# Early attention in buffers that weights take over one by one, a softmax in three instructions, and a scheduler that knows of DVE and GpSimd waiting for each other

## The chip, the cores and the metric

The kernel runs on one core of a Trainium2 chip. The metric is the device time of one execution in microseconds (us). PE is TensorE, DVE is VectorE, ACT is ScalarE, POOL is GpSimd, and SP is the engine from whose queue the kernel issues all its DMAs.

## The reference

Attention of 4 batches, 8 heads, 576 positions and 64 channels feeds two feed-forward layers on 2304 tokens.

```python
# attention: coarse part on means over 4 positions, plus a band of 7 neighbours
out_d = sm_attn(q_d, k_d, v_d)                   # 144 x 144 softmax per head
mask = np.abs(pos[:, None] - pos[None, :]) < 4
attn = softmax(np.where(mask, scale * q @ k.T, -1e9))
x = np.repeat(out_d, 4, axis=2) + attn @ v
# layer 1: RMS norm, gate, value, output (512 -> 1536 -> 512)
xn = x / rms * rms_g
x = (silu(xn @ w_gate) * (xn @ w_val)) @ w_out
# layer 2 (512 -> 2048 -> 512)
x = np.maximum(x @ w_in, 0) ** 2 @ w2_out
```

## The kernel before

No instruction is issued where the code stands. Each call of an engine is recorded as an `Op`; at the end `Plan.trace` puts all records in an order and emits them, which is why every row of the profile has the one line of the emitting call. The order comes from a list scheduler, `Plan.order`: it has a cost in us for each operation (`cost`), a delay between two engines (`lag`), and it alternates between forward and backward passes (`ROUNDS` of them, with a random share of `JIT` in the priorities, drawn from `SEED`), and keeps the order with the earliest end. Some records may run on one of several engines: `VP` on DVE or POOL, `AV` on ACT or DVE; the scheduler chooses. Nothing of this is a time on the chip. Each engine then takes its instructions strictly in the emitted order, and so does the DMA queue of SP.

The string `PLAN` sets in which sequence the parts are recorded:

- `d0` to `d15` (`down`): coarse attention of one batch and two heads. Loads q, k, v; sums over 4 positions on DVE; scores, softmax and output through PE, ACT and DVE. For batches 1 to 3 the result goes to DRAM (`od_d`).
- `a0` to `a5` (`wide`) and `b0` to `b5` (`wide_post`): the band for batch 0, 96 tokens at a time, on PE, with a softmax over 8 heads x 104 keys (tiles `wp`, `wnm`, `wsm`), then the norm into `xh`/`xl`, the input of layer 1.
- `u0` to `u13` and `p2` to `p8`: the band for batches 1 to 3, token rows on partitions: a product of k and q and one of v and the weights per row (tile `pr`, `VP`), summed on DVE; then the norm of a block of 256 tokens.
- `w00` to `w52`: loading and decoding a weight of layer 1. Weights arrive as 64-bit numbers in a staging tile `st` of 512 x 2 words and become two tiles, `hi` and `lo`, so that a product takes three matmuls. One half of a weight is one `decode`: ACT, DVE (two inputs), ACT or DVE, DVE, DVE, POOL or DVE (add), ACT or DVE (`hi`), POOL or DVE (`lo`, a subtraction).
- `x`: one step of layer 1 for a block of 256 tokens and 256 hidden units: 24 matmuls into bank `g`, 24 into `v`, 24 of the step before into `a` or `b`. ACT (`th`, `hh`) and DVE (`th`, `v`, `hl`) stand between them. These matmuls of split numbers are called block matmuls below.

After the last `x` come the weights of layer 2 (32 halves `w2i`, `w2o`) and its steps with 512 tokens.

On-chip memory: a pool `early` holds what the early attention needs (q, k, 7 tiles `wp`, and so on). The pools `late` (6 weights of layer 1 and the staging ring `s`) and `dn` take the same space after the mark `E` in `PLAN`; every first user of a `late` tile waits for every user of `early`. PSUM has 8 banks: tags `a` and `b` with two buffers, `g`, `v`, `t`, `d` with one.

Of the kernel before, what the change touches and what calls it, by code (L numbers as in the profile page):

```python
# [15 lines left out]
I32 = mybir.dt.int32  # L16
# [29 lines left out]
XAB = 2  # L46
DT = 'dbg'
DT1 = ['abt', 'dtd', 'add']
WS = 'aaabbb'
WPT = 'vvvddd'  # L50
WX = 'dtgggb'
WTP = 'ttattt'
VB = 3
PB = 7
NB = 1
DL = 1
EST = 2
SEQ = '011100001101'
PLAN = 'd3 d0 d1 d2 w00 a0 a1 b0 a2 b1 a4 b2 a3 w01 w12 b4 w10 w02 b3 a5 w11 w21 w30 w20 b5 d7 d5 d4 d6 u0 w22 E w31 u1 w32 w41 w40 w42 x x w51 w50 x x x x x x w52 x x x p2 x u2 d8 u3 p3 u4 x d10 x d11 u5 d9 x x x x p4 u6 x x d14 d13 x x d12 x u7 x p5 u8 x d15 x u9 x x x x p6 x x x u10 x u11 x x x p7 x u13 u12 x x x x p8 x x x x x x x x x x x x'
SLOT = [7, 6, 9, 8, 3, 4, 2, 0, 1, 5]  # L60
ROUNDS = 10
LOCK = False
W2ST = 6
# [3 lines left out]
SLACK = 0.02  # L67
JIT = 0.1
SEED = 68976

# [10 lines left out]
def cost(e, method, args, kw, out, ins):  # L81
# [10 lines left out]
    if e in "DQ":  # L92
        return max(0.45, 1.42e-3 * n)
    if e == "A":
# [147 lines left out]
class Op:  # L242


    def __init__(self, n):
        self.n, self.calls, self.cost, self.uses, self.held = n, {}, {}, {}, {}
        self.before, self.after = set(), []

# [11 lines left out]
class Plan:  # L260
# [64 lines left out]
    def record(self, names, method, args, kw):  # L325
# [10 lines left out]
        for e in names:  # L336
            op.calls.setdefault(e, []).append((method, args, kw))
            op.cost[e] = op.cost.get(e, 0.0) + cost(e, method, args, kw, out, ins)
            op.held[e] = e + "S" if LOCK and shared(e, method, kw, out, ins) else op.held.get(e, e)
        for views, writes in ((ins, False), (out, True)):  # L340
# [23 lines left out]
    def order(self, first, forth):  # L364
# [4 lines left out]
        free = defaultdict(lambda: BEGIN if forth else 0.0)  # L369
        done, starts, where, gate = {}, {}, {}, Gate()  # L370

# [18 lines left out]
        while len(done) < len(self.ops):  # L390
# [67 lines left out]
def attn_moe_kernel(ctx: ExitStack, tc, qs, kw, vw, qt, kt, vt, v4, wg, wv, wo, w2i, w2o, gw, gb,  # L458
# [95 lines left out]
    wq, wk, wod = [None] * 4, [None] * 4, [None] * 4  # L554
    qbds = [tile("early", f"qbd{i}", [128, 3, 2, 48]) for i in range(2)]

    def down(b, pr, tags):

        nq, nk = S + SD, S + 8 + SD
        if not late:  # L560
            pool, n = "early", NB
            if b == 0:
                q, k, v4s = (tile("w", f"w{n}", [128, 1024]) for n in (2 * pr, 2 * pr + 1, 8 + pr))
                q, k = q[:, 0:nq], k[:, 0:nk]
                v4s = v4s[0:72].rearrange("p (g d f) -> p g d f", g=4, f=4)
                wq[pr], wk[pr] = q, k
            else:
                q = tile("early", "q", [128, nq], F32, DL)
                k = tile("early", "k", [128, nk], F32, DL)
                v4s = tile("early", "v4s", [72, 4, 64, 4], F32, DL)  # L570
            qbd = qbds[pr % 2]
        else:
            pool, n = "dn", 1
# [3 lines left out]
            qbd = qbds[2]  # L577
# [21 lines left out]
        nm = tile(pool, "nm", [96, 3], F32, 2)  # L599
        V.tensor_reduce(out=nm, in_=sps, axis=AX.X, op=ALU.max, negate=True)  # L600
# [10 lines left out]
        with plan.joint():  # L611
            for h in range(2):
                for qc in range(2):
                    for kc in range(2):
# [29 lines left out]
    def wide(t):  # L644

        v = tile("early", "wv", [WK, DM], F32, VB)
        DQ.dma_start(out=v, in_=vt[WT * t:WT * t + WK])
        p = tile("early", "wp", [WT, 2, 4, WK], F32, PB)
        pt = tile("early", "wpt", [WK, 2, 4, WT], F32, VB)
        bd = band_sb[:, 0 if t == 0 else 2 if t == S // WT - 1 else 1].unsqueeze(1).to_broadcast([WT, 4, WK])  # L650
        sp = [bank(WS[t])[0:WT, 0:4 * WK].rearrange("p (r k) -> p r k", r=4) for h in range(2)]
        with plan.joint():
# [5 lines left out]
        for h in range(2):  # L658
            V.scalar_tensor_tensor(out=p[:, h], in0=sp[h], scalar=SCALE, in1=bd, op0=ALU.mult, op1=ALU.add)
        nm = tile("early", "wnm", [WT, 8], F32, 2)  # L660
        sm_ = tile("early", "wsm", [WT, 8], F32, 2)
        pf = p.rearrange("p h r k -> p (h r) k")
        V.tensor_reduce(out=nm, in_=pf, axis=AX.X, op=ALU.max, negate=True)
        for i in range(8):
            A.activation(pf[:, i], pf[:, i], AF.Exp, bias=nm[:, i:i + 1], accum_out=sm_[:, i:i + 1])
        V.tensor_scalar(out=sm_, in0=sm_, scalar1=1e-9, scalar2=None, op0=ALU.add)
        V.reciprocal(out=sm_, in_=sm_)
        VP.tensor_tensor(out=pf, in0=pf, in1=sm_.unsqueeze(2).to_broadcast([WT, 8, WK]), op=ALU.mult)
        for h in range(2):
            tp = bank(WPT[t])[0:WK, 0:4 * WT].rearrange("p (r k) -> p r k", r=4)  # L670
            with plan.joint():
# [5 lines left out]
    def wide_post(t):  # L677

        pt, v = wx.pop(t)
        x = bank(WX[t])[0:WT]  # L680
        with plan.joint():
# [9 lines left out]
        xa = tile("early", "wxa", [WT, DM], F32, 2)  # L691
        ss = tile("early", "wss", [WT, 1], F32, 2)
# [4 lines left out]
        tp = bank(WTP[t])[:, 0:4 * WT].rearrange("p (k n) -> p k n", k=4)  # L697
        with plan.joint():
# [417 lines left out]
```

## Time and profile before

| | before |
|---|---|
| time, median of 3 runs | 1038.81 us (1036.69 to 1041.39) |
| profiled execution: time | 1037.73 us |
| profiled execution: span from first to last instruction | 1036.0 us |
| mean granted clock of TensorE | 0.958 |
| PE / weight loads of PE | 975.4 us (94%) / 898.2 us (87%) |
| DVE / ACT / POOL | 614.4 (59%) / 414.6 (40%) / 443.8 us (43%) |

The span is 1.7 us shorter than the time of the same execution; the rest lies outside the first and last instruction. The engines' shares are means over stages that have little in common: attention and decoding at first, then matmuls almost alone, with a second stretch of decoding at about 560 to 700 us.

### The profile page before, as it was taken

How to read it: one execution, taken by the hardware profiler on the slowest of the kernel's cores; microseconds unless marked ns; L12 is line 12 of the kernel's file. 1: busy time of each engine (PE TensorE's matmuls, PEld its weight loads, DVE VectorE, ACT ScalarE, POOL GpSimd, SP SyncE). 2: the span in 40 equal slices, each digit the busy share in tenths (PEclk: the TensorE clock that was granted, in tenths of full speed). 3: DMA queues.
4: the chain of work that ended last, by engine and by line, in shares of the span. 5: the costliest groups of instructions: out<-in, count | busy, mean ns of one | idle time of the engine just before them, and what ended most of it. 6: DMA issues, size and time to landing. Idle time of an engine off the chain costs nothing.

```text
span 1036.0 us, 16567 instructions
## 1 busy us (share of the span) xinstructions
PE 975.4 (94%) x6540; PEld 898.2 (87%) x6540; DVE 614.4 (59%) x978; ACT 414.6 (40%) x984; POOL 443.8 (43%) x300
## 2 busy tenths in 40 slices
PE   4688988799999999999999899999999999999998
PEld 4588988799999999999999898777888888888897
DVE  6879999898766767666734578863322322222232
ACT  4678645544334242423223556663222322222222
POOL 0668688995644756568611456861000100000000
PEclk9656999899999999999999999999999999999999
DMA  9735473345343332412010346331100100100010
GB/s 248 200 109 164 134 241 103 100 137 175 102 130 111 93 120 73 127 62 92 27 32 11 133 140 207 99 125 61 72 1 1 52 1 0 41 1 1 1 41 21
DMA packets 38463, 92.89 MB, mean 90 GB/s; under 512 B 4218, under 2 KB 14498, under 8 KB 38386
## 3 DMA queue, kind: packets, MB, share of 16 engines
q1 hardware_dynamic: 38386, 91.84, 28.0%
q8 instruction: 51, 0.84, 0.3%
q14 instruction: 26, 0.21, 0.1%
HBM read 80.62 MB, written 11.21 MB: 89 GB/s over the span
## 4 chain that ended last, share of the span: by engine, by line
PE 61%; DVE 13%; POOL 9%; DMA 7%; issue 4%; ACT 4%; SPq 0%; DVEq 0%; POOLq 0%; ACTq 0%
PE v L454 17%; PE g L454 17%; PE a L454 14%; PE b L454 11%; DVE st L454 6%; POOL st L454 2%; POOL pr L454 2%; POOL w L454 2%; DMA st<-in_w2o 2%; ACT st L454 1%; DVE s L454 1%; DMA k<-in_kw 1%; PE d L454 1%; DMA w<-in_v 1%; DMA st<-in_w2i 1%
## 5 line engine op out<-in xcount | busy, mean ns | idle before, releaser
L454 PE MATMUL g<-xh,w 128*128 128x256 f32 (+1 forms) x1184 | 271.8, 309 | 4.1 <-DVE th L454 4.1
L454 PE MATMUL v<-xh,w 128*128 128x256 f32 (+1 forms) x1040 | 248.2, 316 | 15.6 <-DVE hl L454 14.9
L454 PEld LDWEIGHTS g<-xh,w 128*128 128x128 f32 x1184 | 200.7, 191 | 15.3 <-DVE th L454 5.0
L454 PEld LDWEIGHTS v<-xh,w 128*128 128x128 f32 x1040 | 181.4, 195 | 27.3 <-issue 14.9
L454 PE MATMUL g<-xl,w 128*128 128x256 f32 (+1 forms) x592 | 181.2, 306 | 0.0
L454 PE MATMUL v<-xl,w 128*128 128x256 f32 (+1 forms) x520 | 163.2, 314 | 0.0
L454 DVE SCALAR_TENSOR_TENSOR v<-v,th 128x512 f32<-128x512 f32 (+1 forms) x94 | 63.2, 673 | 134.9 <-ACT th L454 91.6
L454 POOL TENSOR_TENSOR pr<-v,es 128x896 f32<-128x896 f32 x54 | 100.4, 1942 | 68.8 <-DVE es L454 42.3
L454 ACT ACTIVATE th<-g 128x512 f32<-128x512 f32 (+1 forms) x94 | 54.3, 577 | 167.2 <-PE g L454 166.9
L454 PEld LDWEIGHTS g<-xl,w 128*128 128x128 f32 x592 | 113.2, 191 | 5.2
L454 POOL TENSOR_TENSOR pr<-k,q 128x896 f32<-128x896 f32 x49 | 106.5, 2192 | 21.6 <-DVE sc L454 12.9
L454 PEld LDWEIGHTS v<-xl,w 128*128 128x128 f32 x520 | 101.8, 196 | 5.3
L454 POOL TENSOR_TENSOR xl<-st,xh 128x1024 fp32r<-128x1024 f32 (+1 forms) x8 | 16.9, 2125 | 204.3 <-ACT xh L454 204.2
L454 ACT ACTIVATE st<-st 128x512 int32<-128x512 uint32 (+1 forms) x118 | 78.9, 682 | 58.6 <-DVE st L454 31.7
L454 ACT CAST hh<-v 128x512 fp32r<-128x512 f32 (+1 forms) x94 | 53.4, 568 | 109.6 <-DVE v L454 98.6
L454 DVE TENSOR_SCALAR st<-st 128x512 f32<-128x512 f32 (+1 forms) x118 | 87.2, 748 | 8.6 <-ACT st L454 6.7
L454 POOL TENSOR_TENSOR w<-st,w 128x512 fp32r<-128x512 f32 x55 | 78.1, 1427 | 28.7 <-ACT w L454 28.5
L454 PE MATMUL a<-w,hh 128*128 128x512 f32 x320 | 86.7, 392 | 2.4 <-ACT hh L454 2.4
L454 POOL TENSOR_TENSOR st<-st 128x512 int32<-128x512 int32 x59 | 71.1, 1208 | 38.8 <-DVE st L454 36.1
L454 DVE SCALAR_TENSOR_TENSOR g<-g,th 128x512 f32<-128x512 f32 (+1 forms) x40 | 25.8, 644 | 99.6 <-ACT th L454 99.6
L454 DVE TENSOR_TENSOR hl<-v,hh 128x512 fp32r<-128x512 f32 (+1 forms) x94 | 62.3, 663 | 29.2 <-ACT hh L454 26.3
L454 PE MATMUL a<-hh,w 128*128 128x256 f32 x400 | 77.8, 287 | 0.0
(183 smaller groups left out, 1819.1 us busy)
## 6 DMA issues: line engine op xcount, KB each, us to landing
k<-in_kw SPq DMA_DIRECT2D x12, 640.0 KB
v<-in_vw SPq DMA_DIRECT2D x12, 640.0 KB
st<-in_w2i SPq DMA_DIRECT2D x14, 512.0 KB
st<-in_w2o SPq DMA_DIRECT2D x14, 512.0 KB
st<-in_wg SPq DMA_DIRECT2D x11, 512.0 KB
st<-in_wv SPq DMA_DIRECT2D x10, 512.0 KB
st<-in_wo SPq DMA_DIRECT2D x10, 512.0 KB
y<-vv SPq DMA_DIRECT2D x18, 256.0 KB
```

Source lines behind the costliest of these rows:

```text
L454: getattr(self.hw[on[op]], method)(*args, **kw)
```

## The change

Six things change together.

1. `early` and `late` are gone. Sixteen tiles `big` of 128 x 1024 words hold slices of the early attention (`part`); later a pair of them becomes one of the weights 10 to 15 of layer 1 (`SLOT` says which), and four of them the staging ring. A weight waits for the users of its two tiles alone. The working tiles of `down` live in `dn` from the start; its result goes into the tile `pt` and not `pe`. There are 4 tiles `wp`, not 7.
2. The softmax of `wide`: for each of the 6 tiles, 8 ACT instructions (exponential with a bias and a sum) become one subtraction of the maximum over 96 x 832 (`VP`), one exponential over 96 x 832 on ACT and one sum on DVE.
3. PSUM banks are given per record (`TAGS`).
4. `PLAN` and `SLOT` are new.
5. The scheduler's delay after a DMA is 1.9 us, not 1.0, and a DMA's cost goes by its bytes.
6. The scheduler holds that POOL instructions and those DVE instructions that read two operands on chip (or copy at the fast rate) exclude each other except for `HIDE` at their start. `ROUNDS`, `JIT` and `SEED` differ.

```diff
-WPT = 'vvvddd'
...
+TAGS = ('dbg dbg dbg dvg abt abt abd abt dtd dtd dtd dtd add add add add '
+        'aavv aavv aavt bbdd bbdd bbdd gt tt ga gt gt ba')
...
-ROUNDS = 10
-LOCK = False
+ROUNDS = 26
+HIDE = 0.14
...
-JIT = 0.1
-SEED = 68976
+JIT = 0.3
+SEED = 14
...
     if e in "DQ":
-        return max(0.45, 1.42e-3 * n)
+        sb = [v for v in out[:1] + ins[:1] if v.index is not None]
+        return max(0.45, max(size(v) * (v.parts[1] - v.parts[0]) for v in sb) * 4 / 265e3 if sb else 1.0)
...
     if a == "D":
-        return 1.0 if b != "D" else 2.2
+        return 1.9 if b != "D" else 2.2
...
+        def finish(op, e, start, cost):
+
+            return max(start + HIDE, port[0]) + cost - HIDE if e in op.port else start + cost
...
-            done[op] = start + op.time
+            done[op] = finish(op, e, start, op.time)
+            if e in op.port:
+                port[0] = done[op]
...
-    plan.add_pool("early", side="right")
-    plan.add_pool("late", side="right", after=("early",))
-    plan.add_pool("dn", side="right", after=("early",))
+    plan.add_pool("big", side="right")
+    plan.add_pool("dn", side="right")
...
+    big = [tile("big", f"b{i}", [128, 1024], I32 if i in (12, 13) else F32) for i in range(16)]
...
+    wps = [part(i, 0, [WT, 2, 4, WK]) for i in (0, 1, 2, 3)]
+    wpts = [part(i, 0, [WK, 2, 4, WT]) for i in (4, 5, 6)]
...
-        m -= 10
-        return [tile("late", f"w{2 * m + i}", [128, 1024], F32R) for i in range(2)]
+        m = SLOT[m]
+        return [tile("big", f"b{2 * m + i}", [128, 1024], F32R) for i in range(2)]
...
-        if late:
-            od = tile("dn", "pe", [96, 3 * SD], F32, 1)[0:72, 0:256].rearrange("p (c e) -> p c e", c=2)
+        if b:
+            od = tile("dn", "pt", [72, 576])[:, 0:256].rearrange("p (c e) -> p c e", c=2)
...
         V.tensor_reduce(out=nm, in_=pf, axis=AX.X, op=ALU.max, negate=True)
-        for i in range(8):
-            A.activation(pf[:, i], pf[:, i], AF.Exp, bias=nm[:, i:i + 1], accum_out=sm_[:, i:i + 1])
+        VP.tensor_tensor(out=pf, in0=pf, in1=nm.unsqueeze(2).to_broadcast([WT, 8, WK]), op=ALU.add)
+        A.activation(pf, pf, AF.Exp)
+        V.tensor_reduce(out=sm_, in_=pf, axis=AX.X, op=ALU.add)
```

The new order is shown at three places; rows read: operation, tile written<-tiles read, its shape. In the rows of the change the tiles of `big` all read `b_...` with a number, which is also how a PSUM bank of tag `b` reads.

First, PE just ahead of its first block matmul, before:

```order
L454 MATMUL g<-wv,wpt 96x64 x8
L454 MATMUL d<-id,wp 104x96 x4
L454 MATMUL g<-od,up 96x128 x4
L454 MATMUL t<-id,wxa 128x96 x4
L454 MATMUL b<-wv,wpt 96x64 x8
L454 MATMUL a<-k,qbd_86 96x144 x3
L454 MATMUL b<-od,up 96x128 x4
L454 MATMUL t<-id,wxa 128x96 x4
L454 MATMUL v<-xh,w_573 128x256
```

The same place in the change (`b_465` and `b_324` are tiles `wp`, `b_393` is a `wpt` in one row and an `od` in another):

```order
L457 MATMUL g<-b_326,b_393 96x64 x8
L457 MATMUL d<-id,b_465 104x96 x4
L457 MATMUL g<-b_297,b_295 96x128
L457 MATMUL g<-b_393,b_295 96x128
L457 MATMUL g<-b_463,b_295 96x128
L457 MATMUL g<-b_222,b_295 96x128
L457 MATMUL d<-id,b_324 104x96 x4
L457 MATMUL v<-xh,w_623 128x256
```

The first block matmul has moved up: 220 other matmuls stand ahead of it and not 262; the last two `wide_post` now follow it.

Second, POOL from its first work, before:

```order
L454 TENSOR_TENSOR st<-st 128x512 x2
L454 TENSOR_TENSOR pr<-k,q 128x896
L454 TENSOR_TENSOR wp<-wp,wsm 96x832
L454 MEMSET vs 72x4
L454 TENSOR_TENSOR w_373<-st,w_313 128x512
L454 TENSOR_TENSOR pr<-k,q 128x896 x2
L454 TENSOR_TENSOR wp<-wp,wsm 96x832
L454 TENSOR_TENSOR w_373<-st,w_313 128x512
```

And in the change, where `b_244`, `b_324` and `b_384` are tiles `wp` and `b_95` holds the maxima and sums:

```order
L457 TENSOR_TENSOR st<-st 128x512
L457 TENSOR_TENSOR w_258<-st,w_249 128x512
L457 TENSOR_TENSOR b_244<-b_244,b_95 96x832
L457 MEMSET vs 72x4
L457 TENSOR_TENSOR b_176<-b_176 128x512
L457 TENSOR_TENSOR w_258<-b_176,w_249 128x512
L457 MEMSET vs 72x4
L457 TENSOR_TENSOR b_324<-b_324,b_95 96x832
L457 TENSOR_TENSOR b_244<-b_244,b_95 96x832
L457 TENSOR_TENSOR st<-st 128x512
L457 TENSOR_TENSOR pr<-k,q 128x896 x2
```

All six new subtractions stand on POOL, beside the six multiplications that were there.

Third, ACT near the end of layer 1, where the second decoding begins, around the two copies `vv` of the last block, before:

```order
L454 ACTIVATE th<-g 128x512
L454 ACTIVATE st<-st 128x512 x2
L454 COPY vv<-b 128x512 x2
L454 ACTIVATE st<-st 128x512 x3
L454 CAST w_6815<-st 128x512
L454 ACTIVATE st<-st 128x512
L454 CAST hh<-v 128x512
```

The same place in the change:

```order
L457 ACTIVATE th<-g 128x512
L457 CAST w_6674<-st 128x512
L457 COPY vv<-b 128x512 x2
L457 CAST w_6741<-st 128x512
L457 CAST hh<-v 128x512
```

Six steps of decoding that work on a freshly loaded `st` stood between `th` and the next `hh`; none does now.

## Rows read from the trace of the kernel before

**Rows 1.** Part 2 of the page: PE and its granted clock in 40 slices

```profile
PE   4688988799999999999999899999999999999998
...
PEclk9656999899999999999999999999999999999999
```

**Rows 2.** Busy time of each engine in stretches (columns in its first row)

```profile
core 0: us, PE busy (x) PEld busy (x) DVE busy (x) ACT busy (x) POOL busy (x), PEclk, DMA share, GB/s
...
40.00:100.00 60.00, 52.65 (x323) 50.35 (x323) 52.03 (x92) 46.11 (x142) 43.16 (x36) 0.53 0.45 143
100.00:200.00 100.00, 82.25 (x662) 80.60 (x661) 94.85 (x130) 53.96 (x110) 82.05 (x59) 0.93 0.47 151
200.00:260.00 60.00, 58.19 (x492) 57.64 (x491) 52.37 (x87) 28.95 (x83) 45.84 (x29) 1.00 0.45 139
260.00:560.00 300.00, 299.28 (x2554) 298.57 (x2553) 192.67 (x334) 97.58 (x288) 166.22 (x95) 1.00 0.27 84
560.00:640.00 80.00, 75.74 (x584) 73.71 (x583) 55.26 (x79) 45.00 (x77) 40.49 (x33) 0.98 0.40 136
640.00:720.00 80.00, 76.50 (x327) 59.93 (x326) 53.19 (x74) 43.88 (x74) 44.65 (x33) 1.00 0.34 115
720.00:800.00 80.00, 80.00 (x355) 66.24 (x354) 22.22 (x32) 20.62 (x34) 4.75 (x2) 1.00 0.07 24
```

**Rows 3.** Timeline of PE: start, length, line, operation

```profile
93.64 0.56 PE L454 MATMUL v<-xh,w 128*128 128x256 f32 x1
...
199.05 0.28 PE L454 MATMUL v<-xl,w 128*128 128x256 f32 x1
```

**Rows 4.** Waits of PE from 97 to 210 us: total, times, longest

```profile
PE v L454 <- DVE hl L454: 10.4, 4, 6.2
```

**Rows 5.** Tile st on DVE, 100 to 200 us: ns min/median/max

```profile
L454 DVE TENSOR_SCALAR st<-st x34: 400/547/4289, 100.1 to 198.3; 128x512 f32<-128x512 f32 x17, 128x512 int32<-128x512 int32 x17
L454 DVE SCALAR_TENSOR_TENSOR st<-st x15: 654/810/2222, 104.3 to 191.9; 128x512 int32<-128x512 int32 x15
```

**Rows 6.** Groups of DVE, 100 to 200 us: busy, mean ns | idle before

```profile
L454 DVE TENSOR_SCALAR st<-st 128x512 f32<-128x512 f32 x17 | 19.5, 1159 | 0.3 <-ACT st L454 0.2
L454 DVE SCALAR_TENSOR_TENSOR st<-st 128x512 int32<-128x512 int32 x15 | 17.2, 1149 | 0.0
L454 DVE TENSOR_SCALAR st<-st 128x512 int32<-128x512 int32 x17 | 9.8, 585 | 0.0
```

**Rows 7.** Groups of ACT, whole span

```profile
L454 ACT ACTIVATE wp<-wp,wnm 96x104 f32<-96x104 f32 x48 | 17.8, 381 | 2.7 <-DVE rc L454 2.7
L454 ACT ACTIVATION_READ_ACCUMULATOR wp<-wp,wnm 96x1 f32 x48 | 9.6, 200 | 0.0
L454 ACT CAST xh<-st 128x1024 fp32r<-128x1024 f32 x8 | 8.3, 1055 | 1.4 <-DMA st<-y 1.4
```

**Rows 8.** Groups of DVE, whole span

```profile
L454 DVE TENSOR_REDUCE wnm<-wp 96x8 f32<-96x832 f32 x6 | 6.0, 1008 | 0.1
L454 DVE TENSOR_TENSOR pr<-k,q 128x896 f32<-128x896 f32 x5 | 10.1, 2017 | 6.8 <-DMA k<-in_kw 4.7 <-POOL xa L454 2.1
L454 DVE TENSOR_TENSOR xl<-st,xh 128x1024 fp32r<-128x1024 f32 x2 | 4.0, 2014 | 5.6 <-ACT xh L454 5.6
```

**Rows 9.** Groups of POOL, whole span

```profile
L454 POOL TENSOR_TENSOR wp<-wp,wsm 96x832 f32<-96x832 f32 x6 | 10.0, 1659 | 8.2 <-DVE wsm L454 4.7 <-ACT st L454 3.5
L454 POOL TENSOR_TENSOR pr<-k,q 128x896 f32<-128x896 f32 x49 | 106.5, 2192 | 21.6 <-DVE sc L454 12.9 <-DMA k<-in_kw 6.5 <-DVE xa L454 1.3
L454 POOL TENSOR_TENSOR xl<-st,xh 128x1024 fp32r<-128x1024 f32 x6 | 14.3, 2404 | 122.4 <-ACT xh L454 122.4
L454 POOL TENSOR_TENSOR xa<-xa,pr 128x512 f32<-128x512 f32 x12 | 15.6, 1305 | 23.2 <-DMA pr<-od 23.2
```

**Rows 10.** Timeline of ACT: start, length, operation, [idle before and releaser]

```profile
588.51 1.25 ACT L454 ACTIVATE st<-st 128x512 int32<-128x512 uint32 x2 [2.83 <-DMA st<-in_w2i]
592.79 0.59 ACT L454 CAST hh<-v 128x512 fp32r<-128x512 f32 x1 [1.90 <-DVE v L454]
```

More of the change, by code (lines that the diff above doesn't have):

```diff
@@ L246, in __init__ @@
         self.n, self.calls, self.cost, self.uses, self.held = n, {}, {}, {}, {}
-        self.before, self.after = set(), []
+        self.before, self.after, self.port = set(), [], set()
 class Engine:
@@ L338, in record @@
             op.cost[e] = op.cost.get(e, 0.0) + cost(e, method, args, kw, out, ins)
-            op.held[e] = e + "S" if LOCK and shared(e, method, kw, out, ins) else op.held.get(e, e)
+            op.held[e] = e
+            if shared(e, method, kw, out, ins):
+                op.port.add(e)
         for views, writes in ((ins, False), (out, True)):
@@ L369, in order @@
         free = defaultdict(lambda: BEGIN if forth else 0.0)
-        done, starts, where, gate = {}, {}, {}, Gate()
+        done, starts, where, gate, port = {}, {}, {}, Gate(), [0.0]
+        def finish(op, e, start, cost):
+            return max(start + HIDE, port[0]) + cost - HIDE if e in op.port else start + cost
         def enter(op):
@@ L404, in order @@
             if len(where[op]) > 1:
-                end = {o: max(when(o), t, s) + op.cost[o[0]] + SPARE.get(o[0], 0.0) for o, s in where[op].items()}
+                end = {o: finish(op, o, max(when(o), t, s), op.cost[o]) + SPARE.get(o, 0.0) for o, s in where[op].items()}
                 if end[e] > min(end.values()):
@@ L489, in attn_moe_kernel, with part @@
     half_neg = tile("const", "half", [128, 8])
-    gb_sb = tile("early", "gb", [96, DM])
-    band_sb = tile("early", "band", [96, 3, WK])
-    up_sb = tile("early", "up", [72, 3, WT])
+    big = [tile("big", f"b{i}", [128, 1024], I32 if i in (12, 13) else F32) for i in range(16)]
+    def part(i, lo, shape):
+        n = math.prod(shape[1:])
+        v = big[i][0:shape[0], lo:lo + n]
+        names = "abcd"[:len(shape) - 1]
+        if len(names) == 1:
+            return v
+        return v.rearrange(f"p ({' '.join(names)}) -> p {' '.join(names)}", **dict(zip(names, shape[1:])))
+    wps = [part(i, 0, [WT, 2, 4, WK]) for i in (0, 1, 2, 3)]
+    wpts = [part(i, 0, [WK, 2, 4, WT]) for i in (4, 5, 6)]
+    ods = [part(i, 768, [72, 2, 128]) for i in (4, 5, 6, 10)]
+    gb_sb = part(7, 0, [96, DM])
+    wvs = [part(i, n, [WK, DM]) for i, n in ((7, 512), (8, 0), (8, 512))]
+    wxas = [part(9, n, [WT, DM]) for n in (0, 512)]
+    q_sb = big[10][:, 0:S + SD]
+    k_sb = big[11][:, 0:S + 8 + SD]
+    up_sb = part(11, 736, [72, 3, WT])
+    sts = [big[i].rearrange("p (n w) -> p n w", w=2) for i in (12, 13)]
+    v4_sb = part(14, 0, [72, 4, 64, 4])
+    band_sb = part(15, 0, [96, 3, WK])
+    small = [[big[15][0:WT, 320 + 16 * i + 8 * n:328 + 16 * i + 8 * n] for i in range(3)] for n in range(2)]
+    qbds = [part(15, 384, [128, 3, 2, 48]), tile("dn", "qbd", [128, 3, 2, 48])]
     od_d = [tile("dram", f"od{b}", [8 * SD, 128]) for b in range(1, B)]
@@ L524, in staging, with spare @@
             return tile("stage", "st", [128, 512, 2], I32, 3)
+        stages[1] += 1
         if not late:
-            return tile("early", "st", [128, 512, 2], I32, EST)
-        return tile("late", "s", [128, 512, 2], I32, 4)
+            return sts[stages[1] % 2]
+        return spare([128, 512, 2], I32)
+    def spare(shape, dtype):
+        late.append(True)
+        return tile("big", f"b{12 + len(late) % 4}", shape, dtype)
     W1, W2 = {}, {}
@@ L540, in weights1 @@
         n = fp * 3 + m
-        hi, lo = slots(n) if n < 16 else [tile("late", "s", [128, 1024], F32R, 4) for i in range(2)]
+        hi, lo = slots(n) if n < 16 else [spare([128, 1024], F32R) for i in range(2)]
         for n in range(2):
@@ L554, in attn_moe_kernel, with down @@
     wq, wk, wod = [None] * 4, [None] * 4, [None] * 4
-    qbds = [tile("early", f"qbd{i}", [128, 3, 2, 48]) for i in range(2)]
-    def down(b, pr, tags):
+    def down(b, pr):
         nq, nk = S + SD, S + 8 + SD
+        tags = TAGS.split()[4 * b + pr]
         if not late:
-            pool, n = "early", NB
             if b == 0:
@@ L644, in wide @@
     def wide(t):
-        v = tile("early", "wv", [WK, DM], F32, VB)
+        v = wvs[t % len(wvs)]
         DQ.dma_start(out=v, in_=vt[WT * t:WT * t + WK])
-        p = tile("early", "wp", [WT, 2, 4, WK], F32, PB)
-        pt = tile("early", "wpt", [WK, 2, 4, WT], F32, VB)
+        p, pt = wps[t % len(wps)], wpts[t % len(wpts)]
         bd = band_sb[:, 0 if t == 0 else 2 if t == S // WT - 1 else 1].unsqueeze(1).to_broadcast([WT, 4, WK])
-        sp = [bank(WS[t])[0:WT, 0:4 * WK].rearrange("p (r k) -> p r k", r=4) for h in range(2)]
+        tags = TAGS.split()[16 + t]
+        sp = [bank(tags[h])[0:WT, 0:4 * WK].rearrange("p (r k) -> p r k", r=4) for h in range(2)]
         with plan.joint():
@@ L659, in wide @@
             V.scalar_tensor_tensor(out=p[:, h], in0=sp[h], scalar=SCALE, in1=bd, op0=ALU.mult, op1=ALU.add)
-        nm = tile("early", "wnm", [WT, 8], F32, 2)
-        sm_ = tile("early", "wsm", [WT, 8], F32, 2)
+        nm, sm_ = small[t % 2][0:2]
         pf = p.rearrange("p h r k -> p (h r) k")
         V.tensor_reduce(out=nm, in_=pf, axis=AX.X, op=ALU.max, negate=True)
-        for i in range(8):
-            A.activation(pf[:, i], pf[:, i], AF.Exp, bias=nm[:, i:i + 1], accum_out=sm_[:, i:i + 1])
+        VP.tensor_tensor(out=pf, in0=pf, in1=nm.unsqueeze(2).to_broadcast([WT, 8, WK]), op=ALU.add)
+        A.activation(pf, pf, AF.Exp)
+        V.tensor_reduce(out=sm_, in_=pf, axis=AX.X, op=ALU.add)
         V.tensor_scalar(out=sm_, in0=sm_, scalar1=1e-9, scalar2=None, op0=ALU.add)
@@ L690, in wide_post @@
                          stop=True, skip_group_check=True)
-        xa = tile("early", "wxa", [WT, DM], F32, 2)
-        ss = tile("early", "wss", [WT, 1], F32, 2)
+        xa, ss = wxas[t % 2], small[t % 2][2][:, 0:1]
         A.activation(xa, x, AF.Square, accum_out=ss)
@@ L939, in attn_moe_kernel @@
         if c[0] == "d":
-            down(n // 4, n % 4, DT if n < 4 else DT1[n // 4 - 1])
+            down(n // 4, n % 4)
         elif c[0] == "x":
```

42 lines of the change are left out of this document (14 added, 28 removed).

## Prediction, written before the changed kernel was run

> **What bounds the kernel now.** I read the shares of PE over the span first, to see where PE falls short. It has gaps in slices 1 to 8 (up to 207 us), is full from there to the end but for slice 23; its clock is at half speed between about 35 and 107 us and at full speed almost everywhere later [rows 1]. The table of stretches puts numbers on this [rows 2]. From 260 to 560 us PE is busy 299.28 of 300 us, and from 720 to 800 us for all 80: nothing that feeds PE can shorten these. The gaps are elsewhere. From 100 to 200 us PE is busy 82.25 us, so 17.75 us idle; from 200 to 260 us 1.81 us idle; from 560 to 640 us 4.26 us. From 640 to 720 us the idle time reads only 3.50 us, but a matmul counts as busy while it drains, so I take the count: 327 matmuls in 80 us where the full stretch behind it holds 355. The 28 missing ones at 80/355 = 0.225 us each are 6.3 us. I call the first place A (17.75 + 1.81 = 19.6 us) and the second B (4.3 + 6.3 = 10.6 us).
>
> Before A lies the early attention. The first block matmul starts at 93.64 us [rows 3]. From 40 to 100 us PE is busy 52.65 of 60 us at a mean granted clock of 0.53, DVE 52.03 us, ACT 46.11, POOL 43.16 [rows 2]: no engine is the bound alone.
>
> Then I asked what PE waits for in A. The largest wait is for the tile `hl` of DVE, 10.4 us [rows 4]. DVE is busy 94.85 of 100 us there [rows 2], but much of that is no work. The decoding instructions on `st` last between 400 and 4289 ns for the one form and between 654 and 2222 ns for the other, at equal shapes [rows 5]. At their shortest, 34 x 0.40 + 15 x 0.65 = 23.4 us; they took 19.5 + 9.8 + 17.2 = 46.5 us [rows 6]. So DVE stood 23 us inside its own instructions while POOL, busy 82.05 of 100 us [rows 2], used what both share, and `hl` stood behind them in DVE's order.
>
> In B the picture is another. ACT waits 2.83 us for a weight's DMA at 588.51 us with the `hh` that PE needs queued behind it; this `hh` comes at 592.79 us [rows 10]. An instruction that was put too early in the order blocks the ones behind it.
>
> **The softmax of `wide`.** ACT loses 48 exponentials and 48 reads of sums, 17.8 + 9.6 = 27.4 us [rows 7], and gets 6 exponentials over 96 x 832. The trace has none of that shape; the cast over 1024 took 1.055 us [rows 7], scaled to 832 that is an estimate of 0.86 us, 5.1 us for six. ACT is 22 us lighter, all of it before about 100 us. DVE gets 6 sums like `wnm`, 1.008 us each [rows 8]: 6.0 us. The six subtractions all stand on POOL in the new order, and cost what the multiplication by `wsm` costs, 1.66 us [rows 9]: 10.0 us.
>
> **Work that moves from DVE to POOL.** The order has all products `pr` and all 128 x 1024 tiles `xl` on POOL; before, 5 and 2 of them ran on DVE, 10.1 + 4.0 = 14.1 us [rows 8]. On POOL they cost 5 x 2.19 + 2 x 2.40 = 15.8 us [rows 9]. The Trainium skill speaks against this: its "GPSIMD Engine Reference", section 4.1 Engine selection, wants elementwise work with two inputs on VectorE, GpSimd being about half as fast. By that, as an estimate, the seven would cost 28 us on POOL and not 16; the rows show 2192 against 2017 ns for the same product, so here the measurement decides.
>
> **The sum for A.** I counted, engine by engine, what is recorded ahead of the 584th block matmul, which the trace starts at 199.05 us [rows 3], with the mean duration of each group. DVE goes from 184.1 to 180.8 us, POOL from 135.8 to 134.4, ACT from 144.9 to 122.9. The extra work of the softmax is in these sums, and so is what moved ahead of or behind this point. The work of the two loaded engines falls by 1.4 to 3.3 us; I take **-3 us**. PE has 42 fewer small matmuls ahead of its first block matmul (220, not 262); at 52.65/323 = 0.163 us [rows 2] that is 6.8 us sooner at the half clock, but they come later, and DVE sets the pace there too: I count 0, and keep 7 us for the low end.
>
> The order, not the amount, is what the scheduler's new knowledge changes. It no longer puts a DVE instruction that shares with POOL where POOL holds the share. How much of the 19.6 us of idle PE goes away no row shows. At worst nothing; at best all of it, since 23 us of DVE's standing lie under it. The stretch is dense on both engines, which speaks for the lower half: I take 40%, **-8 us**.
>
> **The sum for B.** The work is the same 32 halves. The new order has no decoding step between `th` and `hh` where six stood, and gives a DMA more time before it is counted on. That removes waits like that of 2.83 us; it doesn't make DMA, POOL or DVE faster. Between 0 and 10.6 us I take half, **-5 us**.
>
> **Costs set at nothing.** Taking over buffers one by one lets weights 10 to 15 be decoded earlier, but DVE has no free time from 100 to 200 us to do it in, only 5 us; without that cover it would be part of A's share. The result of `down` in `pt` makes the next copy into `pt`, and not the exponential ahead of it, wait for the store: later by some ACT and PE steps, so no new wait. The PSUM banks and 4 tiles `wp` could add waits on PE before 100 us; ACT's 22 us cover them.
>
> **The forecast.** 1037.73 - 3 - 8 - 5 = 1021.7 us for the profiled execution; the median of the runs shown is 1.1 us above that execution, so **1023 us**.
>
> **Rivals.** First, *the shared access is full and nothing of A comes back*. POOL's 82.05 us and the shortest DVE decoding times, 23.4 us, add up to 105 of 100 us, so no order could pack it better than a few us; POOL's own durations contain waits too, though, so the sum is an upper bound. The Trainium skill states the rule behind it: in "SBUF — State Buffer", section Who interferes with whom, GpSimd and a DVE instruction with two on-chip inputs or at its fast rate exclude each other for the whole instruction. The spread from 400 to 4289 ns agrees. If B's waits only move to another instruction as well, the time is 1038.8 - 3 = 1036 us: no change.
>
> Second, on the other side, *POOL becomes the bound of the early attention*. The subtractions put 10.0 us on POOL between 40 and 100 us, in the chain of each `wide` tile between maximum and exponential: with 43.16 us there it would come to 53 of 60. POOL instructions of the chain then queue behind decoding, the last `wide_post` and so the tokens of layer 1 come later. The whole 10.0 us would end on the first block matmul (104 and not 94 us), and with A and B unchanged the time is 1038.8 + 10 = 1049 us. It decides once POOL reaches some 57 of 60 us in that stretch; ACT's relief and PE's 42 moved matmuls speak against it.
>
> Third, *more than forecast*: the early attention packs better too, PE's first block matmul comes 7 us sooner, and A gives back 15 and B 8 us: 1038.8 - 3 - 7 - 15 - 8 = 1006 us.
>
> **Chances.** The forecast 0.50, the third rival 0.23, the first 0.14, the second 0.13. A difference of 0.5% (5.2 us) is about what a measurement can tell from no change. The forecast and the third rival count as faster (0.73), the first as the same, the second as slower; around their edges I set 0.73, 0.13 and 0.14. The range goes from the third rival's 1006 us, which leaves out what is below it, to 1041 us, which takes in the first and leaves out most of the second. The forecast's own range, with 0 to 15 us from A and 2 to 8 us from B, is 1012 to 1034 us.
>
> **What would show it.** In the profile of the changed kernel: the first block matmul at 88 to 95 us; ACT 20 to 25 us lighter over the span, POOL some 25 us heavier; PE's idle time from 100 to 260 us near 12 us; the decoding instructions on `st` from 100 to 200 us shorter in their mean than 1159 and 585 ns; 341 or more matmuls in a stretch like 640 to 720 us. I am wrong if DVE's decoding instructions stay as long, for then the scheduler's model of the shared access is not the chip's; or if POOL between 40 and 100 us is nearly full and the first block matmul comes after 100 us.

## The result, and the profile after

The changed kernel takes 1004.69 us (median of 4 runs, 1003.07 to 1005.78) where the kernel before took 1039.66 us beside it (4 runs, 1036.69 to 1041.39): a ratio of 0.9665 with an interval of [0.9637, 0.9693]. Its profiled execution took 1003.92 us with a span of 1002.1 us. That is 18 us below the forecast and just under the low end of the range.

The first two parts of its page: engines, then PE and its granted clock in 40 slices.

```profile
PE 964.9 (96%) x6540; PEld 891.3 (89%) x6540; DVE 605.9 (60%) x975; ACT 405.3 (40%) x894; POOL 469.5 (47%) x314
...
PE   5868899999999999999999999999999999999998
...
PEclk9558799999999999999999999999999999999999
```

PE is full from slice 6 to the last but one; the dip of [rows 1] in slice 23 is gone. The stretches, with the columns of [rows 2]:

```profile
40.00:100.00 60.00, 46.45 (x308) 42.27 (x306) 58.15 (x95) 40.32 (x83) 52.27 (x43) 0.64 0.47 153
100.00:200.00 100.00, 95.47 (x786) 94.05 (x786) 96.81 (x136) 55.72 (x114) 83.27 (x57) 0.95 0.46 143
200.00:260.00 60.00, 60.00 (x517) 59.80 (x516) 45.80 (x80) 24.61 (x71) 42.87 (x28) 1.00 0.48 145
260.00:560.00 300.00, 299.78 (x2555) 299.52 (x2554) 191.39 (x341) 108.27 (x306) 181.83 (x104) 1.00 0.29 88
560.00:640.00 80.00, 79.21 (x522) 72.95 (x521) 60.34 (x89) 50.15 (x86) 48.73 (x38) 1.00 0.44 143
640.00:720.00 80.00, 80.00 (x355) 66.26 (x354) 42.59 (x59) 37.06 (x62) 34.73 (x25) 1.00 0.32 102
```

Place A: PE is idle 4.53 us from 100 to 260 us where it was 19.6. Place B: 0.8 us, and 355 matmuls in the second 80 us, none missing. DVE and POOL are no less busy from 100 to 200 us than in [rows 2].

The timeline of PE, first and 584th block matmul, which [rows 3] has at 93.64 and 199.05 us:

```profile
79.01 0.56 PE L457 MATMUL v<-xh,w 128*128 128x256 f32 x1
...
181.55 0.28 PE L457 MATMUL v<-xl,b 128*128 128x256 f32 x1
```

PE's wait for `hl` from 97 to 210 us, the 10.4 us of [rows 4]:

```profile
PE v L457 <- DVE hl L457: 0.7, 1, 0.7
```

The groups of DVE from 100 to 200 us that answer to [rows 6] (decoding also runs in tiles `b` now):

```profile
L457 DVE SCALAR_TENSOR_TENSOR st<-st 128x512 int32<-128x512 int32 x11 | 12.4, 1124 | 0.0
L457 DVE TENSOR_SCALAR st<-st 128x512 int32<-128x512 int32 x12 | 11.8, 982 | 0.0
L457 DVE TENSOR_SCALAR st<-st 128x512 f32<-128x512 f32 x11 | 10.2, 939 | 0.0
...
L457 DVE TENSOR_SCALAR b<-b 128x512 int32<-128x512 int32 x8 | 7.1, 902 | 0.0
L457 DVE SCALAR_TENSOR_TENSOR b<-b 128x512 int32<-128x512 int32 x7 | 7.0, 997 | 0.0
...
L457 DVE TENSOR_SCALAR b<-b 128x512 f32<-128x512 f32 x8 | 6.8, 859 | 0.3 <-ACT b L457 0.3
```

So the wait for `hl` went, but not by shorter decoding: 1149, 585 and 1159 ns became 1124, 982 and 939. With the second staging tile counted in (`s` before, `b` after), the 64 decoding instructions of this stretch mean 958 ns before, and 57 mean 974 ns after. If I sum what each DVE instruction from 100 to 200 us lasts beyond the shortest tenth of its form in the kernel before, DVE stands for 32 us before and 29 after.

To split the gain I use one more mark, the 3400th of 5712 block matmuls, near the end of layer 1 and ahead of B. It starts at 566.8 us before and 545.0 after; from it to the end of the span are 469.2 and 457.1 us. So 21.8 us came ahead of it and 12.1 us behind it.

### The profile page after: what moved, and what is told of

Read it like the earlier page. It is cut to its first block, busy times and chain, and to the rows that moved or that the text cites. A ratio compares the mean times of both kernels' runs of the same rounds, so it can differ in the third digit from the quotient of the medians.

```text
span 1002.1 us, 16469 instructions
## 1 busy us (share of the span) xinstructions
PE 964.9 (96%) x6540; PEld 891.3 (89%) x6540; DVE 605.9 (60%) x975; ACT 405.3 (40%) x894; POOL 469.5 (47%) x314
## 4 chain that ended last, share of the span: by engine, by line
PE 85%; DVE 6%; POOL 3%; DMA 3%; ACT 2%; issue 2%; SPq 0%; DVEq 0%; POOLq 0%; ACTq 0%
PE v L457 24%; PE g L457 24%; PE a L457 19%; PE b L457 16%; DVE b L457 3%; POOL b L457 2%; DVE st L457 1%; PE d L457 1%; POOL w L457 1%; DMA b<-in_wg 1%; PE t L457 1%; ACT b L457 1%; DMA b<-in_wv 1%; DMA st<-in_wo 1%; ACT w L457 1%
## 5 line engine op out<-in xcount | busy, mean ns | idle before, releaser
L457 PE MATMUL g<-xh,w 128*128 128x256 f32 (+1 forms) x776 | 177.1, 308 | 0.0
L457 PE MATMUL v<-xh,w 128*128 128x256 f32 (+1 forms) x632 | 148.9, 314 | 1.4 <-DVE hl L457 1.4
L457 PEld LDWEIGHTS g<-xh,w 128*128 128x128 f32 x776 | 131.6, 192 | 6.4
L457 PE MATMUL v<-xh,b 128*128 128x256 f32 (+1 forms) x552 | 123.5, 303 | 0.1
L457 PE MATMUL g<-xl,w 128*128 128x256 f32 (+1 forms) x388 | 118.8, 306 | 0.0
L457 PEld LDWEIGHTS v<-xh,w 128*128 128x128 f32 x632 | 109.1, 194 | 8.2 <-PE g L457 1.8
L457 PE MATMUL v<-xl,w 128*128 128x256 f32 (+1 forms) x316 | 98.7, 312 | 0.0
L457 PEld LDWEIGHTS v<-xh,b 128*128 128x128 f32 x552 | 93.0, 191 | 4.2 <-DVE hl L457 0.2
L457 PE MATMUL g<-xh,b 128*128 128x256 f32 (+1 forms) x408 | 93.9, 309 | 0.0
L457 PE MATMUL v<-xl,b 128*128 128x256 f32 (+1 forms) x276 | 83.1, 301 | 0.0
```

The lines of the kernel that those rows point to most:

```text
L457: getattr(self.hw[on[op]], method)(*args, **kw)
```

## The experiments

"Knowledge" means points 5 and 6 of the change without the search's numbers: the delay and cost of a DMA, and the exclusion of DVE and POOL. All kernels compute the whole reference. Ratios are to the kernel before in the same batch. The last three columns are of one profiled execution each: start of the 3400th block matmul, time from it to the end, PE's wait for DVE's `hl` from 97 to 210 us ("0": no row for it). A draw is the order that the search ends with for one seed.

| kernel | median us | ratio [95%] | 3400th | rest | `hl` |
|---|---|---|---|---|---|
| before | 1039.66 | 1 | 566.8 | 469.2 | 10.4 |
| after | 1004.69 | 0.9665 [0.9637, 0.9693] | 545.0 | 457.1 | 0.7 |
| a_noport | 1032.87 | 0.9955 [0.9939, 0.9971] | 571.8 | 458.4 | 13.9 |
| a_dmaold | 1022.45 | 0.9855 [0.983, 0.988] | 561.9 | 457.8 | 1.3 |
| a_blind | 1041.85 | 1.003 [1.001, 1.005] | 571.5 | 467.9 | 5.2 |
| a_blind_s15 | 1044.5 | 1.0073 [1.0053, 1.0094] | 574.2 | 468.5 | 12.1 |
| b_model | 1024.08 | 0.987 [0.9841, 0.99] | 563.9 | 457.3 | 10.6 |
| b_model_s14 | 1023.99 | 0.987 [0.9846, 0.9895] | 565.0 | 457.8 | 10.2 |
| b_port | 1029.6 | 0.9904 [0.9871, 0.9936] | 564.0 | 463.6 | 2.4 |
| b_dma | 1028.09 | 0.9897 [0.9863, 0.993] | 563.6 | 461.2 | 13.5 |
| a_seed | 1017.1 | 0.9786 [0.9747, 0.9825] | 558.2 | 457.4 | 3.7 |
| a_seed16 | 1017.39 | 0.9811 [0.9776, 0.9846] | 559.4 | 457.2 | 0 |
| a_oldsearch | 1014.98 | 0.9786 [0.9751, 0.9821] | 555.9 | 457.3 | 0 |
| a_exp8 | 1012.99 | 0.9766 [0.9739, 0.9792] | 554.4 | 456.4 | 4.8 |
| a_exp8_s15 | 1012.21 | 0.9759 [0.9735, 0.9784] | 556.0 | 457.6 | 4.2 |
| a_exp8_s16 | 1014.29 | 0.9769 [0.9726, 0.9812] | 553.1 | 459.2 | 0.6 |
| b_soft | 1039.11 | 1.0015 [0.9994, 1.0036] | 566.3 | 468.5 | 6.0 |
| a_barrier | 1013.08 | 0.9764 [0.9721, 0.9807] | 557.1 | 456.3 | 1.5 |
| a_barrier_s15 | 1018.46 | 0.9823 [0.9802, 0.9843] | 559.4 | 457.0 | 4.8 |
| a_barrier_s16 | 1018.91 | 0.9809 [0.9759, 0.9859] | 561.0 | 456.4 | 0.8 |

**One part of the knowledge taken out of the changed kernel.** First the exclusion (a_noport), then the DMA's numbers (a_dmaold):

```diff
-            if shared(e, method, kw, out, ins):
-                op.port.add(e)
```

> The changed kernel, whose scheduler no longer holds that DVE and GpSimd exclude each other; all else as changed. Theory K (the scheduler's knowledge of the shared access gave most of the 34 us): DVE's decoding instructions between 100 and 200 us wait for GpSimd again, and the time rises by 12 to 25 us, to 1017 to 1030 us, with PE idle again in both decoding stretches. Rival B (buffers that are taken over one by one gave it): at most 5 us, 1005 to 1010 us. Rival S (the softmax in fewer instructions gave it): the same, 1005 to 1010 us.

```diff
-        sb = [v for v in out[:1] + ins[:1] if v.index is not None]
-        return max(0.45, max(size(v) * (v.parts[1] - v.parts[0]) for v in sb) * 4 / 265e3 if sb else 1.0)
+        return max(0.45, 1.42e-3 * n)
...
-        return 1.9 if b != "D" else 2.2
+        return 1.0 if b != "D" else 2.2
```

> The changed kernel with the old cost and delay of a DMA in the scheduler (1.0 us and by elements per row), the exclusion of DVE and GpSimd kept. Theory K in the part that I gave to the second decoding: half-loaded weights block ACT again there, PE loses 5 to 10 us between 540 and 700 us and little before 260 us: 1010 to 1016 us. Rivals B and S: no change, 1003 to 1007 us.

Without the exclusion 28 us of the 35 are lost, without the DMA's numbers 18, nearly all ahead of the 3400th block matmul. Part of that is the draw of the order, as other seeds show below (against those, 16 and 6 us; the 6 lie within the 12 us by which draws differ). The expectation for a_dmaold missed: it had the loss in B, and B stayed closed. In a_noport PE waits for `hl` in A again, 13.9 us, longer than in [rows 4]:

```profile
PE v L455 <- DVE hl L455: 13.9, 5, 6.6
```

**Both taken out** (a_blind), and again with another seed (a_blind_s15):

> The changed kernel with both pieces of the scheduler's new knowledge taken out (no exclusion of DVE and GpSimd, old cost and delay of a DMA); plan, buffers, banks, softmax, passes and seed as changed. Theory K (the knowledge does it): PE is idle in the second decoding again for 8 to 13 us, and the 584th block matmul comes at 200 to 210 us: 1036 to 1046 us, no faster than before. Rival B (buffers, banks and plan have a share of their own in the second decoding): that stretch stays full and the time is 1025 to 1034 us.

> The changed kernel without the scheduler's two new pieces of knowledge, now with seed 15. Theory K: as with seed 14, 1036 to 1046 us, against 1017 us with the knowledge and this seed. Rival L (the draw decides): 1020 to 1030 us.

Nothing of the gain is left, at either seed. B is back as it was in [rows 2]; in a_blind's stretches, and in the waits of PE from 540 to 720 us:

```profile
560.00:640.00 80.00, 77.25 (x613) 74.98 (x611) 49.70 (x75) 42.41 (x73) 35.26 (x28) 1.00 0.40 131
640.00:720.00 80.00, 76.60 (x320) 61.78 (x321) 57.93 (x79) 47.36 (x80) 49.14 (x37) 0.96 0.38 120
```

```profile
PE a L454 <- ACT hh L454: 2.3, 2, 1.6
PE v L454 <- DVE hl L454: 2.0, 3, 1.4
PE a L454 <- DVE hl L454: 1.1, 1, 1.1
PE a L454 <- ACT vv L454: 0.8, 1, 0.8
```

**The knowledge in the kernel before**, and nothing else (b_model; b_model_s14 with the search numbers of the change, `ROUNDS` 26, `JIT` 0.3, `SEED` 14):

```diff
-        return max(0.45, 1.42e-3 * n)
+        sb = [v for v in out[:1] + ins[:1] if v.index is not None]
+        return max(0.45, max(size(v) * (v.parts[1] - v.parts[0]) for v in sb) * 4 / 265e3 if sb else 1.0)
...
-        return 1.0 if b != "D" else 2.2
+        return 1.9 if b != "D" else 2.2
...
+            if shared(e, method, kw, out, ins):
+                op.port.add(e)
...
+            return max(start + HIDE, port[0]) + cost - HIDE if e in op.port else start + cost
```

> The kernel before with the scheduler's two new pieces of knowledge alone (DVE and GpSimd exclude each other; cost and delay of a DMA); plan, buffers, banks, softmax, and the number and seed of the passes as before. Theory K: 15 to 28 us faster than before, 1011 to 1024 us, with PE nearly without idle time in the second decoding. Rivals B and S: within 6 us of before, 1033 to 1041 us.

> The kernel before with the scheduler's knowledge and with the passes, random share and seed of the change. If the knowledge does nearly all that isn't luck, 1012 to 1022 us; if plan, buffers, banks and softmax have a share of their own beside it, it stays at 1022 to 1030 us, as with the old passes.

B closes here too. b_model's stretches:

```profile
560.00:640.00 80.00, 80.00 (x600) 76.99 (x599) 49.23 (x75) 44.30 (x76) 37.30 (x30) 1.00 0.42 134
640.00:720.00 80.00, 79.44 (x349) 65.06 (x349) 54.03 (x75) 45.71 (x76) 51.33 (x36) 1.00 0.40 127
```

Behind the 3400th block matmul it gains 11.9 us; ahead of it only 2 to 3, and PE's wait for `hl` in A stands:

```profile
PE v L464 <- DVE hl L464: 10.6, 5, 4.9
```

**Each part of the knowledge alone in the kernel before:**

> The kernel before with the exclusion of DVE and GpSimd alone added to its scheduler. Theory K: it is the larger piece, 8 to 14 us faster than before in the first decoding and 3 to 8 us in the second: 1020 to 1028 us. If the second decoding needs the DMA's delay, 5 us or more of idle PE stay there.

> The kernel before with the DMA's new cost and delay alone. Theory K: the second decoding gives back 5 to 10 of its 13 us and the first little: 1028 to 1034 us. Rival: without the exclusion of DVE and GpSimd the second decoding stays as it was, 1036 to 1040 us.

Behind the mark the exclusion alone gives 5.6 us and the DMA's numbers alone 8.0; together 11.9. Ahead of it they give 2.8 and 3.2, where the expectation had 8 to 14 for the exclusion. In the changed kernel either of them already gives nearly all of it (458.4 and 457.8 us of rest).

**Other draws of the order.** The changed kernel with seed 15 and 16, and with the search of before (`ROUNDS` 10, `JIT` 0.1, `SEED` 68976):

> The changed kernel with one other seed of the scheduler's random priorities (15, not 14), nothing else. It measures how much of any single comparison is the luck of the draw. Theory K: 1003 to 1010 us. Rival L (the chosen seed carries a large part of the 34 us): 1012 to 1022 us, and then differences of up to 10 us between single orders, such as that of the old softmax, say little about what was edited.

> The changed kernel with a third seed (16). Same readings as for the second: theory K 1003 to 1010 us, rival L 1012 to 1022 us.

> The changed kernel with the passes of before (10 of them, random share 0.1, seed 68976), all else as changed. If the longer search carries weight, 1010 to 1020 us; if not, 1003 to 1010 us.

The three lie within 2.4 us of each other and 10 to 13 us above the kernel with seed 14. The rest behind the mark is 457.1 to 457.4 us in all four; what differs lies ahead of it. Comparisons of single orders below that size say nothing about what lies ahead of the mark (b_port, b_dma and b_soft are one order each), so the next two edits were repeated with three seeds.

**The old softmax in the changed kernel** (seeds 14, 15, 16), and the new one in the kernel before (b_soft):

```diff
-        VP.tensor_tensor(out=pf, in0=pf, in1=nm.unsqueeze(2).to_broadcast([WT, 8, WK]), op=ALU.add)
-        A.activation(pf, pf, AF.Exp)
-        V.tensor_reduce(out=sm_, in_=pf, axis=AX.X, op=ALU.add)
+        for i in range(8):
+            A.activation(pf[:, i], pf[:, i], AF.Exp, bias=nm[:, i:i + 1], accum_out=sm_[:, i:i + 1])
```

> The changed kernel with the old softmax of wide: eight exponentials with sums on ACT for each of the six tiles, no subtraction on GpSimd and no sum on DVE. Rival S: ACT has 22 us more before 100 us and the first block matmul comes 8 to 15 us later: 1013 to 1020 us. Theory K and rival B: GpSimd and DVE are relieved of 10 and 6 us there, ACT has room; 1000 to 1008 us.

> The changed kernel with the old softmax of wide and seed 15. If the new softmax has a share of its own of some 8 us, as seed 14 suggested, 1021 to 1029 us; if that was the draw, 1011 to 1020 us.

> The changed kernel with the old softmax of wide and seed 16. A share of some 8 us of the new softmax: 1021 to 1029 us; the draw: 1011 to 1020 us.

> The kernel before with the new softmax of wide alone. Rival S (ACT's 22 us matter by themselves): 1025 to 1033 us. Theory K: the scheduler that knows nothing of GpSimd and DVE gains nothing from work moved onto both, 1034 to 1046 us.

The mean of the old softmax over three seeds is (1012.99 + 1012.21 + 1014.29) / 3 = 1013.2 us, of the new one (1004.69 + 1017.1 + 1017.39) / 3 = 1013.1. The old one is 8.3 us slower at seed 14, and 4.9 and 3.1 us faster at 15 and 16: an effect of a few us either way is not ruled out. In the kernel before, in one order, it changes nothing either. At seed 14 alone I would have credited it with 8 us.

**The common wait put back**: whoever first takes over a tile `big` waits for all early users of all sixteen, and `w32` is recorded behind the mark:

```diff
+            if pool == "big" and n[0] == 2:
+                self.early = getattr(self, "early", None) or {
+                    u[0] for p, t in self.rings if p == "big" for b in self.rings[p, t][1:] for u in b.uses}
+                ops |= self.early
```

> The changed kernel with the old barrier put back on its buffers: the first new user of any of the sixteen tiles waits for every early user of all sixteen (weight w32 is recorded behind the mark E for that). Rival B (taking over one by one is a main cause): decoding of the weights 10 to 15 starts late, PE is idle for 8 to 20 us between 120 and 180 us, 1013 to 1025 us. Theory K: DVE has no time to decode earlier anyway, 1003 to 1010 us.

> The changed kernel with the old barrier on its buffers and seed 15. If taking buffers over one by one has a share of its own of some 8 us, 1021 to 1029 us; if that was the draw, 1011 to 1020 us.

> The changed kernel with the old barrier on its buffers and seed 16. A share of some 8 us of buffers taken over one by one: 1021 to 1029 us; the draw: 1011 to 1020 us.

Slower by 8.4, 1.4 and 1.5 us than the same seed without it. Two of the three are within what the runs scatter: between nothing and a few us, not settled.

## Why the prediction was wrong

**The direction and the places were right, both sizes too small.** The sum had -11 us for the first block matmul and A, and -5 for B.

| us against before | forecast | after | other draws |
|---|---|---|---|
| to the 3400th block matmul | -11 | -21.8 | -8.6, -7.4, -10.9 |
| from there to the end | -5 | -12.1 | -11.8, -12.0, -11.9 |

**B: the step that failed is "Between 0 and 10.6 us I take half, -5 us".** All of it came, and a little more, 12.1 us. Decoding did not get faster, as said. The tile `st` on POOL from 540 to 720 us, before and then after (columns of [rows 5]):

```profile
L454 POOL TENSOR_TENSOR st<-st x27: 1029/1039/1485, 576.6 to 695.5; 128x512 int32<-128x512 int32 x27
```

```profile
L457 POOL TENSOR_TENSOR st<-st x27: 1036/1160/1489, 545.7 to 681.7; 128x512 int32<-128x512 int32 x27
```

Its 27 halves even spread over 136 us instead of 119, and PE hardly waits. Its waits from 540 to 720 us, before and then after:

```profile
PE v L454 <- DVE hl L454: 3.8, 2, 3.2
PE a L454 <- ACT hh L454: 2.4, 5, 0.8
PE a L454 <- DVE hl L454: 1.6, 2, 1.1
```

```profile
PE v L457 <- DVE hl L457: 0.8, 1, 0.8
```

The wait that the prediction named, ACT held by a weight's DMA with `hh` queued behind it, went as well, from 15.5 to 2.0 us in the same stretch. But in a_dmaold it is 18.0 us, with 457.8 us of rest. The rows before, after, and in a_dmaold:

```profile
ACT st L454 <- DMA st<-in_w2o: 8.0, 8, 1.5
ACT st L454 <- DMA st<-in_w2i: 7.5, 5, 2.8
```

```profile
ACT st L457 <- DMA st<-in_w2i: 1.5, 2, 0.8
ACT st L457 <- DMA st<-in_w2o: 0.5, 1, 0.5
```

```profile
ACT st L456 <- DMA st<-in_w2i: 12.3, 11, 3.8
ACT st L456 <- DMA st<-in_w2o: 5.7, 7, 2.0
```

So ACT's waits for a DMA did not by themselves cost the 12 us; more of PE's waits before were for DVE's `hl` (5.4 us) than for ACT's `hh` (2.4). That it is the place of what PE waits for in the queues fits all this; no run moved a single instruction to show it.

Nothing in B was short of an engine (DVE 55.26, ACT 45.00, POOL 40.49 of 80 us in [rows 2]). By that the waits could go entirely, and halving them had no ground. That the knowledge is the cause, and not the buffers, `PLAN` or banks, is shown from both sides: b_model has it and 457.3 us of rest (457.8 with the other search), a_blind has all but it and 467.9 (468.5 at the other seed).

**A: "It no longer puts a DVE instruction that shares with POOL where POOL holds the share" failed, as its own sign said it would.** I had written that decoding instructions that stay as long would refute it. They did. The `finish` of point 6 says why: it does not hold a DVE instruction back, it adds the standing to the instruction's end. The scheduler counts the standing; it does not forbid it. On PE, in the changed kernel and its variants with the exclusion, the wait for `hl` in A is 0 to 4.8 us, in the three without it 5.2 to 13.9. In the kernel before the two do not go together: 10.6 and 10.2 us with both parts of the knowledge, 2.4 with the exclusion alone, and the mark is at 563.9 to 565.0 us in all three. So how the knowledge acts in A stays open; no run moved `hl` alone. The first rival fell too: DVE and POOL are as full as it said, and PE's idle time still went from 19.6 to 4.53 us.

**A's size: "I take 40%, -8 us" with -3 for the work fits the other draws** (-7.4 to -10.9 for my -11). PE is idle 10.7, 12.2 and 10.7 us from 100 to 260 us in them, near the 12 I gave as the sign. Some 11 to 14 of the 21.8 us is what seed 14 draws beyond them. I had no term and no rival for this, and ended the range at the third rival's 1006 us, whose mechanism (early attention packs better) is the one that came nearest: the first block matmul at 79.01 us, against 84.9 to 86.1 in the other draws and 88 to 95 forecast. An early one is not enough by itself: in b_dma it comes at 69.94 us, and the mark at 563.6.

Where the 21.8 us lie is in the two stretches of PE up to the first block matmul and from there to the mark, before and then after (columns of [rows 2]):

```profile
0.00:93.64 93.64, 66.12 (x433) 60.90 (x433) 72.51 (x128) 60.70 (x198) 46.84 (x43) 0.65 0.65 181
93.64:566.79 473.15, 452.03 (x3797) 448.94 (x3796) 350.44 (x568) 189.74 (x499) 302.17 (x187) 0.98 0.33 105
```

```profile
0.00:79.01 79.01, 55.16 (x361) 48.99 (x361) 71.59 (x113) 43.53 (x90) 54.06 (x46) 0.66 0.66 199
79.01:545.04 466.03, 457.41 (x3869) 454.37 (x3868) 348.32 (x583) 199.82 (x521) 318.40 (x198) 0.98 0.36 112
```

PE's idle time falls by 3.7 us in the first and 12.5 us in the second, and its busy time in both together by 5.6 us; the sum's -8 us stood for the second alone. Its term for the moved matmuls, "I count 0", also rests on a wrong price: 0.163 us is that of a matmul of the trace, where 432 and then 360 stand ahead of the first block matmul (one recorded matmul is one or two there; the 433 and 361 of the rows hold the first block matmul too). 72 fewer make 11.7 us and not 6.8; PE's busy time ahead of it falls by 11.0. Part of that is spent again behind it: up to the 584th there are 188 small matmuls where there were 106.

**What stays open in A.** On the 3400th block matmul the knowledge gives 2 to 3 us in the kernel before, and in the changed one 12 to 29 (545.0 to 559.4, from 571.5 and 574.2; at equal seeds 26 and 16). So it seems to need something else of the change; but the kernel before without the knowledge was run in one order only (b_soft, with the new softmax, is at 566.3), and part of the difference can be that order's draw. It is, by more than some us, neither the softmax nor the common wait, for those variants with the old part are at 553.1 to 561.0. `PLAN`, `SLOT`, the banks and the layout of the tiles are left; they depend on each other and were not separated. By the medians all but the knowledge is worth 7 to 9 us: 1024 us with the knowledge in the kernel before, 1015 to 1017 in the other draws.

**The smaller terms.** POOL is 25.7 us heavier, as said (some 25), and the second rival's point was not reached: 52.27 us of 60 from 40 to 100 us, and the first block matmul came earlier. ACT is only 9.3 us lighter, not 20 to 25, though the durations of its instructions add up to 22.7 us less. I had added durations of neighbours that overlap on one engine: the 27.4 us of [rows 7] keep ACT busy 19.09 us, in the stretch of tile `wp` on ACT in the kernel before:

```profile
core 0: us, ACT busy (x), PEclk, DMA share, GB/s
0.00:100.00 100.00, 19.09 (x96) 0.66 0.64 182
```

The new groups of the softmax in the changed kernel, on ACT, DVE and POOL (`b` stands for `wp`, `wnm` and `wsm`):

```profile
L457 ACT ACTIVATE b<-b 96x832 f32<-96x832 f32 x6 | 5.4, 897 | 7.2 <-POOL b L457 7.1
...
L457 DVE TENSOR_REDUCE b<-b 96x8 f32<-96x832 f32 x12 | 11.9, 1004 | 0.7 <-ACT b L457 0.7
...
L457 POOL TENSOR_TENSOR b<-b,b 96x832 f32<-96x832 f32 x12 | 22.7, 1906 | 1.9 <-DVE b L457 1.9
```

ACT's 897 ns and DVE's 1004 ns are close to the 0.86 us and 1.008 us of the sum; POOL's twelve mean 1906 ns where I had used 1659 [rows 9]. The new exponentials keep ACT busy 5.4 us, so the softmax takes 13.7 us off it; that 9.3 are left is because ACT's other instructions, equal in their sum (441.8 and 441.6 us), overlap less. None of it shows in the time beyond the draw.

The reading that POOL does the product `pr` about as fast as DVE (2192 against 2017 ns) is wrong. DVE's five in the kernel before, and POOL's 49:

```profile
L454 DVE TENSOR_TENSOR pr<-k,q x5: 1092/1922/2998, 34.1 to 478.8; 128x896 f32<-128x896 f32 x5
```

```profile
L454 POOL TENSOR_TENSOR pr<-k,q x49: 2069/2126/3027, 34.2 to 506.3; 128x896 f32<-128x896 f32 x49
```

The mean of DVE's five holds standing, as that of the decoding does. Shortest against shortest, POOL takes 2069 ns and DVE 1092, so about half as fast is what this trace shows too.

## What to carry to other kernels

Where PE waited for engines with time to spare (B), a scheduler with truer delays took all of the wait; where DVE was nearly full (A) somewhat under half went in three draws and most of it in one. Let the range reach up to the whole wait. When a search draws the order, one draw is one sample (here 12 us wide): repeat an edit over several seeds before crediting it, draw the kernel before again too, and let a forecast's range hold the draw. A mean that holds standing is no price: take the shortest of the form beside it. Engine time saved is the drop of busy time in a stretch, not the sum of durations of instructions that overlap.

## What the runs showed of the hardware

TensorE's granted clock early on cost nothing that the time shows. Two draws of the changed kernel, a_seed and then a_seed16 (columns: PE, PEld, DVE, ACT, POOL, clock):

```profile
20.00:40.00 20.00, 13.01 (x112) 11.14 (x110) 20.00 (x32) 10.48 (x22) 12.71 (x11) 0.65 0.96 261
...
40.00:100.00 60.00, 45.67 (x254) 41.92 (x255) 57.23 (x79) 33.19 (x63) 49.62 (x38) 0.50 0.41 126
```

```profile
20.00:40.00 20.00, 17.63 (x128) 15.06 (x127) 17.47 (x34) 9.90 (x20) 14.80 (x12) 1.00 0.89 255
...
40.00:100.00 60.00, 41.77 (x257) 38.12 (x257) 54.41 (x81) 35.09 (x70) 50.90 (x40) 0.98 0.42 132
```

From 40 to 100 us one runs at 0.50, which is the 1.2 GHz level, the other at 0.98, nearly all of it at 2.4 GHz; ahead of it PE had been busy 13.01 and 17.63 of 20 us. PE needs 45.67 against 41.77 us for 254 and 257 matmuls, and the medians are 1017.1 and 1017.39 us: DVE is busy 57.23 and 54.41 of 60 us, so it seems to set the pace there. These are two orders; one order shows the same: of the four executions of a_seed16 one had a mean granted clock of 0.988 and took 1018.39 us, the others 0.956 to 0.960 and 1016.97 to 1017.55 us. Here the half clock under a stage that another engine holds was no loss to be won back.
